# Dealing tokens to partitions in turns of five and four, and moving the left-out-token tables to the last expert

## The chip, the cores and the metric

The kernel runs on one core of a Trainium2 chip. The metric is the device time of one execution in microseconds (us). Before the change three runs gave 597.97 us at the median, between 597.38 and 598.83. A core has a matmul engine (TensorE, PE in the profile, with its weight loads as PEld), a vector engine (DVE), a scalar engine (ACT), GpSimd (POOL) and a sync engine (SP, here used to issue DMA), and 16 DMA engines that all queues share. A difference of about 0.2%, some 1.2 us, is the least that a measurement of this kernel can tell from no change.

## What is computed

A linear attention without softmax, then a top-1 mixture of experts over its output (shapes: 8 batches, 8 heads, 576 tokens a batch, 64 columns a head; 8 experts, 512 to 1,024 and back; a capacity of 1,152 tokens an expert):

```
kv = einsum('bhsd,bhse->bhde', k, v)
out = einsum('bhsd,bhde->bhse', q, kv)
x = out / sqrt(mean(out*out, -1) + 1e-6) * g_norm        # one row of 512 for each of 4,608 tokens
e = argmax(x @ w_gate);  g = softmax(x @ w_gate)[e]      # one expert and one gate for a token
pos = how many earlier tokens chose the same expert       # kept while pos < capacity
y[token] = g * (relu(x @ w1[e]) @ w2[e])                  # 0 for a token that is not kept
```

The position counts tokens in the order of their index, so whatever place a token has in the chip's memory, its index must be known there.

## The kernel before

**Attention.** One batch has 576 = 128 x 4.5 tokens. The kernel gives a batch C = 5 columns on 128 partitions. Column 0 holds tokens 0 to 63 on partitions 0 to 63 (the other half of the column is zero, written once by a memset), columns 1 to 4 hold tokens 64 to 575, four in a row on each of the 128 partitions. k, v and q of half the heads (four of eight) are one load, six loads a batch and 48 in all. `load` issues each as two DMAs on SP's queue:

```
nc.sync.dma_start(h.t[:, :, 1:C], src[b, hs, HP:S].rearrange("h (p c) d -> p h c d", c=C - 1))
nc.sync.dma_start(h.t[0:HP, :, 0], src[b, hs, 0:HP].rearrange("h p d -> p h d"))
```

The first moves 512 pieces of 1,024 bytes, the second 256 pieces of 256 bytes; the pieces are the packets of the profile. Nine buffers (three each for k, v, q) are reused in turn, and every DMA also waits for the one eight before it on its queue. `kv_products` (L700) makes k'v of a batch, `unit` turns q (L764) and multiplies it with kv (L782), `squares` and `route` norm the rows, choose experts and count positions; `place` (L931) counts with ten small matmuls against a triangle `tri16`, `upto16` or `ones16`. `write` (L999, L1001) sends the rows with their logits to `x_dram` from POOL's queue, in two DMAs of 64 and 128 partitions. From batch 3 on the weights of one early expert are loaded and split into a high and a low fp16 part, and the first 384 of its tokens are computed, beside the attention.

**Experts.** For each expert r, `weights` loads w1 and w2 into `raw1` and `raw2`, takes their largest element (DVE `am` L330, `a` L338; a transpose on PE, `across`, L343; DVE `bm` L347; a broadcast on PE, `back`, L350; DVE `bmax` to `sg`), and splits them with that scale (ACT `w1h`, `w2h` L364; DVE `w1l`, `w2l` L370). `rows_beside` gathers the token rows of the next expert (POOL `xg` L426, `xm` L434, ACT `pair` L458, POOL `pair` L462, a DMA transpose from SP), and DVE copies their gates (`gt` L439, which waits for the gather). `products` runs the first GEMM in eight blocks (PE `hp` L515, ACT `hh` L520, DVE `hl` L523), `second` the second one (PE `yp` L561 and L570, ACT `ysb` L586, POOL `out_dram` L591).

**What sets the order.** `Plan` is a small list scheduler in the kernel file: every step has a planned duration, its engines, its dependencies and a key; steps are placed on engines by earliest start and then by key, and the instructions are written in that order. On the chip each engine runs its own list strictly in order. So a step that is placed early on DVE stands ahead of everything placed later, whether or not someone waits for it.

**Left-out tokens.** A fixed budget of rows is computed for each expert. `plan_rest` (L1301 to L1419) makes tables of what a budget or the capacity leaves out, in some 55 small DVE steps; `rest` reads one number from them at the very end and, if it is above zero, runs extra tiles. The steps form one chain on DVE with no dependency ahead of the first, at the key of the last expert:

```
steps, o = plan_rest(), None
for _ in range(60):
    o = op(("V", 0.2), lambda e: next(steps, None), [o], key + 1)
```

Of the kernel before, what the change touches and what calls it, by code (L numbers as in the profile page):

```python
# [11 lines left out]
F32 = mybir.dt.float32  # L12
I32 = mybir.dt.int32
AF = mybir.ActivationFunctionType
ALU = mybir.AluOpType
# [13 lines left out]
NIO = 3  # L29
# [128 lines left out]
def attention_moe_kernel(  # L158
# [12 lines left out]
    nc = tc.nc  # L171
    NB, H, S, D = q.shape
# [3 lines left out]
    P = 128  # L176
    C = 5
    HP = P // 2
    HH = H // 2
    KD = DM // P  # L180
    KF = F // P
    XW = D + E
# [4 lines left out]
    cst = ctx.enter_context(tc.tile_pool(name="cst", bufs=1))  # L187
# [5 lines left out]
    x_dram = dram.tile([N, XR], F32, name="x_dram")  # L193


# [7 lines left out]
    tok_i = cst.tile([P, 2, NT], I32, name="tok_i")  # L203
    by_col = lambda i: tok_i[:, i].rearrange("p (b c) -> p b c", c=C)
    nc.gpsimd.iota(by_col(0), [[S, NB], [1, C]], base=HP, channel_multiplier=C - 1)
    nc.gpsimd.iota(by_col(0)[:, :, 0:1], [[S, NB], [0, 1]], base=1, channel_multiplier=1)
    tok1 = cst.tile([P, NT], F32, name="tok1")
    nc.vector.tensor_copy(tok1, tok_i[:, 0])
# [28 lines left out]
    nc.vector.memset(desc[HP:P, 0], 0.0)  # L237
# [15 lines left out]

    wgs = cst.tile([P, 2, 2, 2, E], F32, name="wgs")
# [5 lines left out]


    kv_bds = []
    for i in range(2):
        t = cst.tile([P, H, 2, XW], F32, name=f"kv_bd{i}")
        nc.gpsimd.memset(t, 0.0)
        kv_bds.append(t)
# [365 lines left out]
    actx = ExitStack()  # L632
    io = actx.enter_context(tc.tile_pool(name="io", bufs=1))
# [6 lines left out]

    ios = {}
    for i in range(NIO):
        for nm, eng in (("k", nc.gpsimd), ("v", nc.vector), ("q", nc.gpsimd)):
            flat = io.tile([P, HH * C * D + D], F32, name=f"{nm}_sb{i}")
            t = flat[:, 0:HH * C * D].rearrange("p (h c d) -> p h c d", h=HH, c=C)
            eng.memset(t[HP:P, :, 0], 0.0)
            if nm == "q":
                eng.memset(flat[:, HH * C * D:], 0.0)
            ios[nm, i] = t, flat
# [21 lines left out]
    def load(b):  # L671
        ts = {}
        for j, (nm, half) in enumerate(ORDER):
            h = new(nm)
            h.t, h.flat = ios[nm, (len(rings[nm].holds) - 1) % NIO]

            def go(e, h=h, src={"k": k, "v": v, "q": q}[nm], hs=slice(half * HH, (half + 1) * HH)):
                nc.sync.dma_start(h.t[:, :, 1:C], src[b, hs, HP:S].rearrange("h (p c) d -> p h c d", c=C - 1))
                nc.sync.dma_start(h.t[0:HP, :, 0], src[b, hs, 0:HP].rearrange("h p d -> p h d"))

            o = op(("S", ISSUE), go, [], (b - 2) * C + j * 0.8, takes=(h,))
            ts[nm, half] = h, op(("D", LOAD), None, [o], takes=(), uses=(h,))
            issued.append(o)
        return ts
# [136 lines left out]
    def route(b, oh, ssh, outs, sums):  # L821
# [26 lines left out]
        o = V(0.1, guess, [o])  # L848
# [74 lines left out]
        def place(e):  # L923
# [4 lines left out]
            terms += [(tri16, rep(ohe[:, c], max(c, 1)), min(c, 1), c + 1) for c in range(C)]  # L928
            terms += [(upto16 if c else ones16, rep(ohe[:, c], C - 1 - c), c + 1, C) for c in range(C - 1)]
# [66 lines left out]
        def write(first):  # L996
            def go(e):
                if first:
# [615 lines left out]
    for r in range(E):  # L1614
# [48 lines left out]
```

## Time and profile before

| | us |
|---|---|
| median of three runs | 597.97 |
| the profiled execution, own time | 593.89 |
| its span, first to last instruction | 592.1 |
| PE busy | 542.7 |
| DVE busy | 384.1 |
| ACT busy | 257.7 |
| POOL busy | 224.0 |

Busy time is the sum over the instructions of an engine. Times of day in the text count from the span's start. The profiled execution is 4.08 us shorter than the median of the runs; a sum made in its rows is taken over to the median as a difference. In the views of the trace, "idle before <- X" is how long an engine stood before an instruction and what ended that, the chain of waits is the work that ended last followed back from the end, and DMA share is the busy time of the 16 DMA engines over the stretch (it can be above 1, since packets overlap).

### The profile page before, as it was taken

To read this page: it belongs to the slowest core of one execution; us is meant where nothing else is said; L and a number is where in the kernel's file an instruction comes from. 1 tells how busy PE (TensorE), PEld (TensorE's weight loads), DVE (VectorE), ACT (ScalarE), POOL (GpSimd) and SP (SyncE) were. 2 spreads that over 40 slices of the span, in tenths; PEclk is the share of its full clock that TensorE was granted. 3 is DMA by queue.
4 is the path that set the end of the run, shared out by engine and by line. 5 is a ranking of instruction groups with operands and counts; after the bars stand their busy time and mean duration, and the time that the engine had idled before them with its cause. 6 is when DMAs were issued, how large, how long until landed. Compare 5 with 4: busy or idle time off the path is not lost.

```text
span 592.1 us, 11996 instructions
## 1 busy us (share of the span) xinstructions
PE 542.7 (92%) x4535; PEld 373.8 (63%) x4535; DVE 384.1 (65%) x1026; ACT 257.7 (44%) x500; POOL 224.0 (38%) x273
## 2 busy tenths in 40 slices
PE   2887999788988979999899999999999999999996
PEld 2787898687534545654575467477558648747843
DVE  2386687999976998899999665648638625201200
ACT  1565676588502652471825252443526435211211
POOL 6002243165334785517522722463274173011011
PEclk9999999988998997999899999999999999999999
DMA  8999999936239669777763752856386143001000
GB/s 225 288 292 329 323 313 356 339 115 232 91 129 346 161 135 244 184 234 228 188 245 103 192 164 90 217 108 216 101 176 206 50 105 73 1 37 38 1 37 29
DMA packets 94654, 102.71 MB, mean 173 GB/s; under 512 B 51650, under 2 KB 76226, under 8 KB 93568
## 3 DMA queue, kind: packets, MB, share of 16 engines
q1 hardware_dynamic: 86528, 70.50, 44.3%
q0 software_dynamic: 8064, 31.40, 15.4%
q8 instruction: 37, 0.61, 0.4%
q14 instruction: 25, 0.20, 0.1%
HBM read 73.20 MB, written 20.68 MB: 159 GB/s over the span
## 4 chain that ended last, share of the span: by engine, by line
PE 41%; DVE 19%; DMA 15%; issue 14%; POOL 4%; ACT 3%; SPq 2%; POOLq 0%; DVEq 0%; ACTq 0%
PE hp L515 17%; PE yp L561 12%; DMA out_dram<-ysb,si 5%; PE op L782 3%; DVE w1l L370 3%; DMA q_sb<-in_q_dram 3%; DVE am L330 3%; DMA v_sb<-in_v_dram 3%; DMA xs<-pair 2%; DMA xg<-x_dram,gi 2%; DVE w2l L370 2%; PE qp L764 2%; PE yp L570 2%; DVE hl L523 2%; PE a L700 2%
## 5 line engine op out<-in xcount | busy, mean ns | idle before, releaser
L515 PE MATMUL hp<-xs,w1h 128*128 128x320 f16 (+6 forms) x960 | 137.1, 296 | 1.6 <-DVE hl L523 0.7
L515 PEld LDWEIGHTS <-w1h 128*128 128x128 f16 x1024 | 100.5, 99 | 38.9 <-issue 4.2
L561 PEld LDWEIGHTS <-hh 128*128 128x128 f16 x560 | 54.2, 98 | 63.7 <-issue 1.9
L591 POOL DMA_INDIRECT out_dram<-ysb,si x42 | 44.7, 1064 | 130.8 <-ACT ysb L586 94.1
L520 ACT ACTIVATE hh<-hp 128x320 f16<-128x320 f32 (+7 forms) x64 | 40.9, 640 | 110.7 <-PE hp L515 108.9
L426 POOL DMA_INDIRECT xg<-x_dram,gi x42 | 43.7, 1040 | 92.5 <-DVE w1l L370 58.2
L330 DVE TENSOR_REDUCE am<-raw 128x1 f32<-128x512 f32 x120 | 75.4, 673 | 0.0
L523 DVE SCALAR_TENSOR_TENSOR hl<-hp,hh 128x320 f16<-128x320 f32 (+7 forms) x64 | 47.4, 741 | 41.0 <-ACT hh L520 40.9
L515 PE MATMUL hp<-xs,w1l 128*128 128x320 f16 (+6 forms) x480 | 72.1, 292 | 0.0
L561 PE MATMUL yp<-w2h,hl 128*128 128x512 f16 x272 | 65.9, 385 | 0.0
L561 PE MATMUL yp<-w2h,hh 128*128 128x512 f16 x272 | 64.9, 379 | 0.8 <-ACT ysb L586 0.8
L782 PE MATMUL op<-kv_bd,qt 128*128 128x144 f32 (+1 forms) x384 | 60.2, 301 | 5.8 <-ACT o_sb L665 2.1
L561 PE MATMUL yp<-w2l,hh 128*128 128x512 f16 x272 | 64.7, 379 | 0.0
L515 PEld LDWEIGHTS <-w1l 128*128 128x128 f16 x512 | 49.9, 98 | 16.6
L782 PEld LDWEIGHTS op<-kv_bd,qt 128*128 128x128 f32 x384 | 52.3, 202 | 9.1 <-ACT o_sb L665 3.3
L458 ACT CAST pair<-xm 128x512 f16<-128x512 f32 (+5 forms) x36 | 22.1, 614 | 81.0 <-POOL xm L434 73.9
L370 DVE SCALAR_TENSOR_TENSOR w2l<-raw,sw,w2h 128x512 f16<-128x512 f32 x64 | 47.6, 793 | 7.7 <-ACT w2h L364 7.7
L462 POOL TENSOR_TENSOR pair<-xm,pair 128x512 f16<-128x512 f32 (+5 forms) x36 | 43.4, 1207 | 23.1 <-ACT pair L458 22.7
L370 DVE SCALAR_TENSOR_TENSOR w1l<-raw,sg,w1h 128x512 f16<-128x512 f32 x64 | 52.0, 853 | 0.0
L586 ACT ACTIVATE ysb<-yp,ysc 128x512 f32<-128x512 f32 (+5 forms) x41 | 27.9, 681 | 51.5 <-PE yp L561 36.7
L561 PEld LDWEIGHTS <-hl 128*128 128x128 f16 x280 | 27.7, 99 | 34.2 <-issue 2.6
L434 POOL TENSOR_TENSOR xm<-xg 128x512 f32<-128x512 f32 (+5 forms) x39 | 43.4, 1114 | 9.6 <-DMA xg<-x_dram,gi 6.1
(242 smaller groups left out, 690.9 us busy)
## 6 DMA issues: line engine op xcount, KB each, us to landing
raw<-in_moe_w_dram SPq DMA_DIRECT2D x64, 512.0 KB
x_dram<-o_sb POOLq DMA_DIRECT2D x8, 1152.0 KB
k_sb<-in_k_dram SPq DMA_DIRECT2D x16, 512.0 KB
v_sb<-in_v_dram SPq DMA_DIRECT2D x16, 512.0 KB
q_sb<-in_q_dram SPq DMA_DIRECT2D x16, 512.0 KB
x_dram<-o_sb POOLq DMA_DIRECT2D x8, 144.0 KB
k_sb<-in_k_dram SPq DMA_DIRECT2D x16, 64.0 KB
v_sb<-in_v_dram SPq DMA_DIRECT2D x16, 64.0 KB
```

Of the source, the lines that this page charges most:

```text
L330: nc.vector.tensor_reduce(out=am()[:, p:p + 1], in_=raw[:, sl(p)], axis=AX.X, op=ALU.max, apply_absolute_value=True)
L370: nc.vector.scalar_tensor_tensor(out=wl[:, sl(p)], in0=raw[:, sl(p)], scalar=z["s"], in1=wh[:, sl(p)], op0=ALU.mult, op1=ALU.subtract)
L426: nc.gpsimd.indirect_dma_start(out=self.xg[i][0:n], out_offset=None, in_=x_dram[0:self.rows, :], in_offset=bass.IndirectOffsetOnAxis(ap=se ...
L434: eng.tensor_tensor(out=self.xm[i][0:n].rearrange("p (h d) -> p h d", h=H), in0=xg[:, :, 0:D], in1=xg[:, :, D:D + 1].broadcast_to([n, H, D ...
L462: nc.gpsimd.tensor_tensor(out=pair[0:n, 1], in0=self.xm[i][0:n], in1=pair[0:n, 0], op=ALU.subtract)
L515: nc.tensor.matmul(self.view(hp)[:, u], lhsT=w[:, c, j * P:(j + 1) * P], rhs=x[:, c, u * hw:(u + 1) * hw], start=(t == 0 and c == 0), stop ...
L520: nc.scalar.activation(self.out(self.hh, j), self.view(hp), AF.Relu)
L523: nc.vector.scalar_tensor_tensor(out=self.out(self.hl, j), in0=self.view(hp), scalar=0.0, in1=self.out(self.hh, j), op0=ALU.max, op1=ALU.s ...
L561: nc.tensor.matmul(yp[0:n, 0:DM], lhsT=h[:, j, o:o + n], rhs=w[:, j, :], start=(m == 0), stop=(m == len(self.terms) - 1))
L586: nc.scalar.activation(self.ysb[0:n], yp[0:n, 0:DM], AF.Copy, scale=self.ysc[0:n, i:i + 1])
L591: nc.gpsimd.indirect_dma_start(out=out[:, :], out_offset=bass.IndirectOffsetOnAxis(ap=self.sidx[0:n, col:col + 1], axis=0), in_=ysb[0:n], ...
L782: nc.tensor.matmul(ph.t[:, j * m:(j + 1) * m], lhsT=qt.t[:, i * P:(i + 1) * P], rhs=x, start=True, stop=True)
```

## The change

**Tokens.** Each pair of partitions now takes nine tokens in a row: the even partition five, the odd one four, in columns 1 to 4, with its column 0 zero. A load is again two DMAs on SP, over the 64 odd partitions (256 pieces of 1,024 bytes) and the 64 even ones (256 pieces of 1,280 bytes); the rows go to `x_dram` in the same two groups. Token numbers, the mask `desc` and the triangle matmuls follow the new order. The zeros of column 0 are now written over all 128 partitions, in front of the first load, which has to wait for them; the buffers' memsets are therefore moved to the head of the program.

**Tables.** The chain of `plan_rest` now depends on `hh[0]`, the first hidden block of the last expert.

```diff
-            eng.memset(t[HP:P, :, 0], 0.0)                       # behind the set-up
+            eng.memset(t[:, :, 0], 0.0)                          # ahead of it
...
-                nc.sync.dma_start(h.t[:, :, 1:C], src[b, hs, HP:S].rearrange("h (p c) d -> p h c d", c=C - 1))
-                nc.sync.dma_start(h.t[0:HP, :, 0], src[b, hs, 0:HP].rearrange("h p d -> p h d"))
+                rows = src[b, hs].rearrange("h (p n) d -> p h n d", n=2 * C - 1)
+                nc.sync.dma_start(h.t[1:P:2, :, 1:C], rows[:, :, C:])
+                nc.sync.dma_start(h.t[0:P:2], rows[:, :, 0:C])
...
-            terms += [(tri16, rep(ohe[:, c], max(c, 1)), min(c, 1), c + 1) for c in range(C)]
-            terms += [(upto16 if c else ones16, rep(ohe[:, c], C - 1 - c), c + 1, C) for c in range(C - 1)]
+            terms += [(tri16, rep(ohe[:, c], c + 1), 0, c + 1) for c in range(C)]
+            terms += [(upto16, rep(ohe[:, c], C - 1 - c), c + 1, C) for c in range(C - 1)]
...
-                    nc.gpsimd.dma_start(x_dram[b * S:b * S + HP], o_sb[0:HP, 0].rearrange("p h x -> p (h x)"))
+                    nc.gpsimd.dma_start(rows[:, C:], o_sb[1:P:2, 1:C].rearrange("p c h x -> p c (h x)"))
...
-                    nc.gpsimd.dma_start(x_dram[b * S + HP:(b + 1) * S].rearrange("(p c) d -> p c d", c=C - 1),
-                                        o_sb[:, 1:C].rearrange("p c h x -> p c (h x)"))
+                    nc.gpsimd.dma_start(rows[:, 0:C], o_sb[0:P:2].rearrange("p c h x -> p c (h x)"))
...
-            steps, o = plan_rest(), None
+            steps, o = plan_rest(), hh[0]
```

Three places in the instruction order carry the prediction. The first is SP's queue at the start of the program: the loads of the first k and v halves, with what each waits for (49 is the end of a semaphore's name; the number behind k_sb is the buffer's). Before:

```order
L678 DMA k_sb_180<-in_k_dram 128x4x256
L679 DMA k_sb_180<-in_k_dram 64x4x64
L678 DMA v_sb_182<-in_v_dram 128x4x256
L679 DMA v_sb_182<-in_v_dram 64x4x64
L678 DMA k_sb_187<-in_k_dram 128x4x256
```

Now:

```order
L684 DMA k_sb_73<-in_k_dram 64x4x256
L685 DMA k_sb_73<-in_k_dram 64x4x320 [waits Pool_49]
L684 DMA v_sb_75<-in_v_dram 64x4x256
L685 DMA v_sb_75<-in_v_dram 64x4x320 [waits DVE_49]
L684 DMA k_sb_80<-in_k_dram 64x4x256
```

The number and order of the DMAs is the same; the second of a load waits for a memset on POOL or DVE.

The second is DVE where it takes the maxima of the fourth expert's weights (the second and third experts are under way): `am`, `a`, `bm` and `sg` are steps of that maximum, `gt` waits for a gather, and `sel`, `big`, `off` and `t_tab` belong to the tables. Before:

```order
L439 COPY gt<-xg 128x1
L330 TENSOR_REDUCE am_3816<-raw_2643 128x1
L1354 TENSOR_TENSOR sel<-iota_77,upto 128x396
L347 TENSOR_REDUCE bm<-pt_max 1x1
...
L1372 SCALAR_TENSOR_TENSOR t_tab<-iota_77,t_tab 128x44
L370 SCALAR_TENSOR_TENSOR w1l_2645<-raw_149,sg,w1h_2644 128x512
L347 TENSOR_REDUCE bm<-pt_max 1x1
L370 SCALAR_TENSOR_TENSOR w1l_2645<-raw_149,sg,w1h_2644 128x512 x4
```

Now:

```order
L456 COPY gt<-xg 128x1
L364 TENSOR_REDUCE bm<-pt_max 1x1
L347 TENSOR_REDUCE am_3792<-raw_2651 128x1
L456 COPY gt<-xg 112x1
...
L355 TENSOR_REDUCE a_1_3872<-am_3792 128x1
L387 SCALAR_TENSOR_TENSOR w1l_2653<-raw_181,sg,w1h_2652 128x512 x3
L364 TENSOR_REDUCE bm<-pt_max 1x1
L387 SCALAR_TENSOR_TENSOR w1l_2653<-raw_181,sg,w1h_2652 128x512 x3
```

The table steps are gone from here; the first `bm` stands right behind the `gt` that waits for the gather, the second `bm` behind three `w1l` instead of one. On POOL, two output writes change places with an `xm` each there; on PE, the broadcast that needs the first `bm` stands eight matmuls earlier.

The third is DVE in the last expert, between the blocks of its first GEMM (`hl`). Before:

```order
L552 TENSOR_SCALAR ysc<-gt,ys 128x4
L552 TENSOR_SCALAR ysc<-gt,ys 32x1
L523 SCALAR_TENSOR_TENSOR hl<-hp,hh 128x544 x7
L576 COPY yt<-yp 128x128
L1422 TENSOR_LOAD n_i
```

Now:

```order
L1360 TENSOR_TENSOR sel<-iota_101,upto 128x396
L540 SCALAR_TENSOR_TENSOR hl<-hp,hh 128x544
L1362 TENSOR_TENSOR big<-iota_101,upto 128x396
L1364 TENSOR_TENSOR sel<-sel,big 128x396
L1370 SCALAR_TENSOR_TENSOR off<-upto,start 128x9
L1372 SCALAR_TENSOR_TENSOR off<-ent,off 128x9
L1374 TENSOR_TENSOR big<-sel,off 128x396
L1376 TENSOR_REDUCE t_tab<-big 128x44
L1378 SCALAR_TENSOR_TENSOR t_tab<-iota_101,t_tab 128x44
L540 SCALAR_TENSOR_TENSOR hl<-hp,hh 128x544
```

The chain of table steps now stands among these seven blocks, five to nine steps in a gap; the last two steps stand behind them. The gap that holds the most work is the one with the seven steps from `big` to `t_tab`.

## Rows read from the trace of the kernel before

**Rows 1.** The page, its head and busy times.

```profile
span 592.1 us, 11996 instructions
PE 542.7 (92%) x4535; PEld 373.8 (63%) x4535; DVE 384.1 (65%) x1026; ACT 257.7 (44%) x500; POOL 224.0 (38%) x273
```

**Rows 2.** Busy time by stretch (columns PE, PEld, DVE, ACT, POOL, clock, DMA).

```profile
30.00:40.00 10.00, 9.33 (x131) 8.76 (x131) 8.36 (x25) 6.57 (x16) 0.00 (x0) 0.97 1.14 292
...
290.00:310.00 20.00, 20.00 (x150) 14.45 (x149) 19.70 (x41) 9.57 (x15) 4.91 (x5) 1.00 0.82 253
```

**Rows 3.** The chain of waits, first 75 us (start, us, what).

```profile
18.40 7.66 DMA v_sb<-in_v_dram
26.20 1.71 PE a L700 x40
...
49.46 7.74 DMA q_sb<-in_q_dram
...
59.98 10.19 DMA q_sb<-in_q_dram
70.30 0.63 PE qp L764 x4
```

**Rows 4.** DMA queue from 20.5 to 21 us (packets, MB, share).

```profile
DMA packets 152, 0.15 MB, mean 309 GB/s; under 512 B 1, under 2 KB 152, under 8 KB 152
q1 hardware_dynamic: 152, 0.15, 108.9%
```

**Rows 5.** The same from 21.4 to 21.9 us.

```profile
DMA packets 250, 0.15 MB, mean 301 GB/s; under 512 B 152, under 2 KB 249, under 8 KB 249
q1 hardware_dynamic: 249, 0.13, 112.0%
```

**Rows 6.** The same from 103.5 to 106 us, weight loads.

```profile
DMA packets 370, 1.03 MB, mean 410 GB/s; under 512 B 32, under 2 KB 149, under 8 KB 370
q1 hardware_dynamic: 370, 1.03, 102.3%
```

**Rows 7.** The first instructions, timeline (start, us, engine, line, what).

```profile
1.23 0.74 SPq L679 DMA_DIRECT2D k_sb<-in_k_dram  x1
...
6.27 0.31 POOL L646 MEMSET k_sb<- 64x256 f32 x1
```

**Rows 8.** Who PE waited for, 185 to 592 us (us, times, longest).

```profile
PE yp L581 <- DVE t_e L1315: 4.7, 1, 4.7
PE pt_max L350 <- DVE bm L347: 3.0, 2, 2.7
PE hp L515 <- DVE hl L523: 0.7, 1, 0.7
```

**Rows 9.** DVE's timeline, 275 to 285 us.

```profile
275.35 0.15 DVE L439 COPY gt<-xg 128x1 f32<-128x1 f32 x1 [1.17 <-DMA xg<-x_dram,gi]
...
276.02 0.56 DVE L1354 TENSOR_TENSOR sel<-iota,upto 128x396 f32<-128x396 f32 x1
276.50 0.27 DVE L347 TENSOR_REDUCE bm<-pt_max 1x1 f32<-1x128 f32 x1
...
283.63 0.73 DVE L1372 SCALAR_TENSOR_TENSOR t_tab<-iota,t_tab 128x44 f32<-128x44 f32 x1
```

**Rows 10.** PE's timeline in the same place.

```profile
276.82 0.38 PE L350 MATMUL pt_max<-bm,ones 1*128 1x1 f32 x2 [0.30 <-DVE bm L347]
...
285.27 0.38 PE L350 MATMUL pt_max<-bm,ones 1*128 1x1 f32 x2 [2.68 <-DVE bm L347]
```

**Rows 11.** POOL's timeline in the same place.

```profile
276.62 1.01 POOL L591 DMA_INDIRECT out_dram<-ysb,si  x1 [2.39 <-DMA out_dram<-ysb,si]
277.65 1.08 POOL L434 TENSOR_TENSOR xm<-xg 128x512 f32<-128x512 f32 x1
```

**Rows 12.** ACT's timeline in the same place.

```profile
282.48 3.17 ACT L364 ACTIVATE w1h<-raw,sg 128x512 f16<-128x512 f32 x5
```

**Rows 13.** DVE's timeline in the last expert.

```profile
555.03 0.72 DVE L523 SCALAR_TENSOR_TENSOR hl<-hp,hh 128x544 f16<-128x544 f32 x1 [2.06 <-ACT hh L520]
```

More of the change, by code (lines that the diff above doesn't have):

```diff
@@ L193, in attention_moe_kernel @@
     x_dram = dram.tile([N, XR], F32, name="x_dram")
+    actx = ExitStack()
+    io = actx.enter_context(tc.tile_pool(name="io", bufs=1))
+    ios = {}
+    for i in range(NIO):
+        for nm, eng in (("k", nc.gpsimd), ("v", nc.vector), ("q", nc.gpsimd)):
+            flat = io.tile([P, HH * C * D + D], F32, name=f"{nm}_sb{i}")
+            t = flat[:, 0:HH * C * D].rearrange("p (h c d) -> p h c d", h=HH, c=C)
+            eng.memset(t[:, :, 0], 0.0)
+            if nm == "q":
+                eng.memset(flat[:, HH * C * D:], 0.0)
+            ios[nm, i] = t, flat
     ident = cst.tile([P, P], F32, name="ident")
@@ L236, in attention_moe_kernel @@
     nc.vector.tensor_copy(desc, desc8.rearrange("p (o e) -> p o e", o=1).broadcast_to([P, C, E]))
-    nc.vector.memset(desc[HP:P, 0], 0.0)
+    even = cst.tile([P, 1], F32, name="even")
+    nc.vector.tensor_scalar(out=even, in0=pair[:, 0:1], scalar1=-1.0, scalar2=1.0, op0=ALU.mult, op1=ALU.add)
+    nc.vector.tensor_scalar(out=desc[:, 0], in0=desc8, scalar1=even, scalar2=None, op0=ALU.mult)
     rbud = cst.tile([P, E], F32, name="rbud")
@@ L252, in attention_moe_kernel @@
         nc.gpsimd.dma_start(gcol[h2 * D:(h2 + 1) * D], g_norm.rearrange("(d o) -> d o", o=1))
+    kv_bds = []
+    for i in range(2):
+        kv_bds.append(cst.tile([P, H, 2, XW], F32, name=f"kv_bd{i}"))
+    for t in kv_bds:
+        nc.gpsimd.memset(t, 0.0)
     wgs = cst.tile([P, 2, 2, 2, E], F32, name="wgs")
@@ L259, in attention_moe_kernel @@
     nc.vector.tensor_scalar(out=wgs, in0=wgs, scalar1=gcol, scalar2=None, op0=ALU.mult)
[L262 to L266, printed above, removed]
     mv_all = cst.tile([P, NT], F32, name="mv_all")
@@ L629, in slots @@
         return both
-    actx = ExitStack()
-    io = actx.enter_context(tc.tile_pool(name="io", bufs=1))
     at = actx.enter_context(tc.tile_pool(name="at", bufs=2))
@@ L639, in attention_moe_kernel @@
     tab, misc = bank("tab"), bank("misc")
[L641 to L645, printed above, removed]
-            eng.memset(t[HP:P, :, 0], 0.0)
-            if nm == "q":
-                eng.memset(flat[:, HH * C * D:], 0.0)
-            ios[nm, i] = t, flat
     o_sbs, sss = [], []
@@ L997, in go @@
             def go(e):
+                rows = x_dram[b * S:(b + 1) * S].rearrange("(p n) d -> p n d", n=2 * C - 1)
                 if first:
-                    nc.gpsimd.dma_start(x_dram[b * S:b * S + HP], o_sb[0:HP, 0].rearrange("p h x -> p (h x)"))
+                    nc.gpsimd.dma_start(rows[:, C:], o_sb[1:P:2, 1:C].rearrange("p c h x -> p c (h x)"))
                 else:
-                    nc.gpsimd.dma_start(x_dram[b * S + HP:(b + 1) * S].rearrange("(p c) d -> p c d", c=C - 1),
-                                        o_sb[:, 1:C].rearrange("p c h x -> p c (h x)"))
+                    nc.gpsimd.dma_start(rows[:, 0:C], o_sb[0:P:2].rearrange("p c h x -> p c (h x)"))
             return go
```

13 lines of the change are left out of this document (9 added, 4 removed).

## Prediction

> **What bounds the kernel now.** I read the busy times first: PE works 542.7 of 592.1 us [rows 1], so apart from PE's own work only some 50 us can be won, and the question is where they lie. Busy time by stretch answers that for both ends. In 30 to 40 us the DMA engines are full (share 1.14 at 292 GB/s) and PE still has gaps, while from 290 us on PE is busy for all of its time [rows 2]: what this change removes there is worth nothing, and what it adds costs only if PE is made to wait. The chain of waits then says which loads count. Up to the `v` half whose DMA is issued at 18.40 and done 7.66 us later, at 26.06, the loads set the pace; its end is what PE's next products start from [rows 3]. From there to 49.46 the chain runs over PE and DVE, then it enters two more `q` loads (7.74 and 10.19 us from issue to landing), and from 70.30 on no load stands in it [rows 3]. The list of those for whom PE waits after 185 us holds one large item, 4.7 us for a step `t_e` of the tables, and 3.0 us in two pieces for `bm` [rows 8].
>
> **Loads: what one costs.** A load is 589,824 bytes (128 x 4 x 1,024 + 64 x 4 x 256); at 292 GB/s that is 2.02 us, and 10 loads have landed by 26.06. The change keeps the bytes and turns 512 packets of 1,024 and 256 of 256 bytes into 256 of 1,024 and 256 of 1,280. So I need a price for each size. A stretch with 152 packets of 1,024 bytes has a share of 108.9% of 16 engines over 0.5 us, 8.71 us of engine time, or 57.3 ns a packet [rows 4]. The next has 97 of these and 152 small ones in 112.0%, 8.96 us; less 97 x 57.3 it leaves 3.40 us, 22.4 ns a small one [rows 5]. Weight loads have 221 of 4,096 bytes, 117 taken at 57.3 and 32 at 22.4 in 102.3% of 2.5 us, 40.92 us: 152 ns for 4,096 bytes [rows 6]. The price of another byte is therefore 0.045 ns between 256 and 1,024 bytes and 0.031 above it. A packet of 1,280 bytes, which this trace does not have, comes to 65 to 69 ns. Before, a load holds each engine for (512 x 57.3 + 256 x 22.4) / 16 = 2.19 us, after it for (256 x 57.3 + 256 x 65 to 69) / 16 = 1.96 to 2.02: 0.17 to 0.23 us less, and over a share of 1.12 to 1.14 (packets overlap) 0.15 to 0.21 us of time. I take 0.15, the price nearest to the 1,024-byte row. The ends: nothing, if the bytes and not the packets set the 2.02 us; 256 x 22.4 / 16 / 1.12 = 0.32, if the small packets go and 256 further bytes on a packet are free. That 4,096-byte packets move 410 GB/s [rows 6] speaks against the lower end.
>
> The row of small packets says that one takes 0.39 of the time of a 1,024-byte packet for a quarter of its bytes [rows 5]. [...]
>
> **Loads: how many count.** Ten up to 26.06, then those that land in the two stretches of the chain. 7.74 us are 3.8 loads of 2.02; the second stretch holds 2.45 us more, in which `x_dram` rows of the first batch share the queue, and otherwise as many. The first load of each has been running for a part of its time when the chain enters, so I count 3.5 for each, 7 for both. That is 17 x 0.15 = **2.6 us** (ends 0 and 5.4). Loads between 28 and 47 us land while PE and DVE set the pace, so they are costed at nothing.
>
> **The start.** The first `k` half no longer needs zeros behind it but ahead of it: its second DMA waits for a memset, a wait that holds SP's queue and with it all later loads. The memsets, which now begin only at 6.27 on POOL (0.31 us each) [rows 7], stand at the head of the program; the first is done about when the second DMA of the load was issued, 1.23 [rows 7]. I cost it at 0, with 0.3 us (one memset) to either side. What they push back on POOL, the identity and the gate weights, is wanted only after 15 us. The `x_dram` writes keep their bytes in packets that are all above 9,000 bytes, and the wider triangle matmuls are a few columns: both 0.
>
> **Tables: what they held up.** The steps moved stand on DVE between 184 and 333 us. At the fourth expert's maxima eight of them, from `sel` (0.56) at 276.02 to `t_tab` (0.73) at 283.63, sum to 5.9 us [rows 9]; behind the last stands the `bm` for which PE waits 2.68 us [rows 10]. A sum that stopped here would book 2.68. But what is late next? In the new order the second `bm` stands behind three `w1l`, which need `w1h`; ACT begins these at 282.48, five in 3.17 us [rows 12], so the third ends at 284.4 and its `w1l` near 285: no gain at all as the times stand. `w1h` waits for a cast behind POOL's output write, which stood 2.39 us for the write before it, with `xm` behind [rows 11]. The new order puts an `xm` ahead of that write, which frees the casts by about 1.6 us (1.01 of the write and part of its wait). So the second `bm` wins about **1.5 us**.
>
> The first `bm` stands right behind `gt`, which waited 1.17 us for its gather and ran at 275.35 [rows 9]. PE's broadcast, which came to it at 276.52 and waited 0.30 [rows 10], stands eight matmuls earlier, and PE will be there some 1.7 us sooner. The gather does not move with it. Small savings before this place (`hl` 0.7 and the first `bm` 0.30 [rows 8, 10], and some 0.4 of `yp`'s 4.7, the table step that the list names last; the rest of the 4.7 is `w2l` on DVE, which stays) are 1.4 us, and a new wait of about 1.8 us here eats them. I book the two at 0 together. The ends for the tables: 2.68 + 1.4, about 4 us won, if gather and casts come with PE; 0.7 us lost, if the new wait stands whole against half of the small savings and the second `bm` wins nothing.
>
> **Tables: where they go.** In the last expert `hl` runs every 2.78 us for 0.72 us, and DVE is idle 2.06 us between [rows 13]. The gap from `big` to `t_tab` has seven steps, 3.1 us if `big`, `off` and `t_tab` run like their neighbours of the same shape, 5.3 us as they ran beside POOL (POOL has nothing but seven issues there). So `hl` can come 1.1 us late, but it is read only by the second GEMM and by the buffer of a block two further on, which leaves about 1.4 us: 0, with 1.8 us at the worst price. The last two steps are behind the last `hl`, with PE's second GEMM still to run.
>
> **Sum.** 2.6 + 1.5 = 4.1 us less: 593.89 becomes 589.8 in the profiled execution, and, as a difference, 597.97 becomes **593.9**.
>
> **The rivals.**
> *(A) The loads do not get shorter*, because bytes set their pace, or because the hardware cuts 1,280 bytes into 1,024 and 256, in which case the packets are those of before and the change does not do what it says. For it: the share is above 1 all through [rows 2], so a packet's time is partly queueing. Against it: the rows of larger packets. It gives 597.97 - 1.5 = 596.5. [...]
> *(B) The tables' gain is lost whole:* the broadcast waits for the gather, the second `bm` for three `w1l`, as long as before. For it: the rows of `gt` and `w1h` [rows 9, 12]. Against it: POOL's new order. 597.97 - 2.6 = 595.4.
> *(C) Slower: packets that begin at multiples of 256 bytes cost more.* The pieces now start every 2,304 bytes, no longer every 1,024. If each costs what a large and a small one cost together, 79.7 ns, a load holds an engine 2 x 256 x 79.7 / 16 = 2.55 us in place of 2.19, 0.32 us more over the share: 17 x 0.32 = 5.4 us lost, less 1.5: 601.9. It decides once a packet of 1,280 and one of 1,024 bytes take over 137 ns together (2 x 57.3 + 22.4); in the sum they take 122 to 126. Against it: before, the 256-byte packets and large ones side by side show no such price [rows 5].
> *(D) Both gains in full:* 5.4 + 4, 588.6.
>
> **How the numbers follow.** The forecast has 0.45, A 0.17, B 0.18, C 0.10, D 0.10. A difference of 0.2%, 1.2 us, is about what a measurement of this kernel can tell. The forecast gives 0.40 faster, 0.04 the same, 0.01 slower; A, 1.5 us under the old median, is split 0.08, 0.07 and 0.02; B 0.12, 0.06 and 0 (the start and the last expert can cost it its margin); C all slower; D all faster: 0.70, 0.17 and 0.13. The range leaves out C and the edge of D and takes in A with 1.8 us of the last expert and the start's 0.3 on top: 588.5 to 599.5.
>
> **What would show it.** Up to 26 us: the last of ten loads done near 24.6, and engine time of a load near 2.0 us; 26.1 says A, over 28 says C. No table step on DVE before 540 us; the second `bm`'s broadcast with a wait near 1 us and the first with one near 1.8. In the last expert `hl` late by up to a microsecond, and no wait of PE. PE busy without a gap from 290 on. It would be wrong if SP stood waiting for a memset, if casts still held the second `bm`, or if the new order put some wait elsewhere among the second to fourth experts, where DVE's, POOL's and PE's lists are dealt anew.

## The result

The changed kernel takes 591.36 us at the median of nine runs (589.6 to 594.63), the kernel before 597.97 in nine runs beside it (596.29 to 599.99). The ratio is 0.9894 with a 95% interval of 0.9872 to 0.9915, 5.1 to 7.7 us less. The forecast was 593.9 with a range of 588.5 to 599.5, and faster with a chance of 0.70. The direction and the range held and the gain was 6.6 us where 4.1 were forecast, but three of the steps that led to it were wrong, and that the sum came this near is in part luck. The rest of the text is about these. Ratios leave out executions more than 1.5% above the fastest of their kernel; medians leave out none.

The head of the page of after (first line the span, then busy time of each engine), which answers to [rows 1]:

```profile
span 588.8 us, 12003 instructions
PE 540.6 (92%) x4535; PEld 373.1 (63%) x4535; DVE 382.6 (65%) x1031; ACT 258.0 (44%) x500; POOL 221.5 (38%) x273
```

All busy times are as before to within 2.5 us. Of the 3.3 us by which the span is shorter, 2.1 are PE's own busy time, although it runs the same 4,535 matmuls; the rest is waiting that went. Over whole executions the clock that was granted to TensorE is the same (as a share of the full clock, a median of 0.978 in 63 executions of the kernel before over all series, 0.976 in 15 of the changed one), so it does not carry the gain; between two single traces it can, as a place below shows. This execution took 590.7 us, 0.7 under its median; that of before lay 4.1 under its own. Two traces set side by side therefore show only 3.2 us, and small differences are read below from several of each kind.

Busy time by stretch (PE, PEld, DVE, ACT, POOL, clock, DMA share, GB/s), the same two stretches as [rows 2]:

```profile
30.00:40.00 10.00, 8.09 (x130) 7.33 (x129) 8.97 (x35) 5.92 (x16) 0.00 (x0) 1.00 1.00 324
290.00:310.00 20.00, 20.00 (x148) 14.34 (x147) 17.85 (x38) 4.32 (x7) 4.12 (x5) 1.00 0.41 139
```

The DMA engines move 324 GB/s where they moved 292, with a lower share; the late stretch is full of PE as it was. For whom PE waits on loads up to 185 us (us in all, times, longest), in before:

```profile
PE a L700 <- DMA v_sb<-in_v_dram: 4.0, 2, 2.0
PE qp L764 <- DMA q_sb<-in_q_dram: 3.9, 3, 2.3
```

and in after:

```profile
PE misc L937 <- DVE ohe L913: 3.8, 4, 1.9
PE a L706 <- DMA v_sb<-in_v_dram: 1.8, 1, 1.8
```

7.9 us of waiting for loads became 1.8; the `q` loads are no longer waited for at all, and what took their place in part is `ohe`, a step of the routing on DVE (1.9 us before). From 185 us on PE's waits of after are these (line numbers are 17 higher than before's here):

```profile
PE yp L598 <- DVE gt L456: 5.8, 1, 5.8
PE pt_max L367 <- DVE bm L364: 2.5, 2, 2.1
PE hp L532 <- DVE p2t L312: 1.3, 2, 0.9
```

Against [rows 8], the 4.7 us before `yp` are now 5.8, and the two waits for `bm` are 2.5 in place of 3.0. The place on which the prediction booked 1.5 us, the second `bm`, gave 0.5 (2.68 became 2.14).

### The profile page after: what moved, and what is told of

Same layout as the page of the kernel before. It is cut to its first block, busy times and chain, and to the rows that moved or that the text cites. A ratio compares the mean times of both kernels' runs of the same rounds, so it can differ in the third digit from the quotient of the medians.

```text
span 588.8 us, 12003 instructions
## 1 busy us (share of the span) xinstructions
PE 540.6 (92%) x4535; PEld 373.1 (63%) x4535; DVE 382.6 (65%) x1031; ACT 258.0 (44%) x500; POOL 221.5 (38%) x273
## 4 chain that ended last, share of the span: by engine, by line
PE 38%; issue 17%; DVE 16%; DMA 10%; POOL 5%; ACT 4%; POOLq 0%; SPq 0%; DVEq 0%; ACTq 0%
PE hp L532 19%; PE yp L578 8%; DMA out_dram<-ysb,si 8%; PE op L788 4%; DVE w1l L387 3%; DVE w2l L387 3%; DVE am L347 2%; PE qp L770 2%; POOL pair L479 2%; DVE hl L540 1%; DMA xg<-x_dram,gi 1%; PE a L706 1%; PE yp L587 1%; POOL xm L451 1%; DMA raw<-in_moe_w_dram 1%
## 5 line engine op out<-in xcount | busy, mean ns | idle before, releaser
L532 PE MATMUL hp<-xs,w1l 128*128 128x320 f16 (+6 forms) x480 | 72.1, 292 | 0.0
L578 PE MATMUL yp<-w2h,hl 128*128 128x512 f16 x272 | 64.3, 379 | 0.0
```

Of the source, the lines that this page charges most:

```text
L532: nc.tensor.matmul(self.view(hp)[:, u], lhsT=w[:, c, j * P:(j + 1) * P], rhs=x[:, c, u * hw:(u + 1) * hw], start=(t == 0 and c == 0), stop ...
L578: nc.tensor.matmul(yp[0:n, 0:DM], lhsT=h[:, j, o:o + n], rhs=w[:, j, :], start=(m == 0), stop=(m == len(self.terms) - 1))
```

## Where the time went, over several traces

PE runs the same 4,535 matmuls in all these kernels, in nearly the same order, so the start of the n-th matmul is a clock that can be compared. Taken from the traces, the time from the span's start to matmul 720 (k, v and q of the first batches), from there to 1,560 (end of the attention), to 2,640 (the first experts), to 4,080 and to the last, in us:

```
                              to 720   to 1560   to 2640   to 4080   to the last
before                         76.07    103.79    171.11    186.88     48.36
before, second trace           77.65    104.09    172.54    188.21     47.59
before + tables moved          77.18    104.14    168.82    189.37     47.59
after, tables not moved        75.56    103.54    174.45    190.73     47.59
after                          71.75    105.32    168.40    189.05     48.29
after, second trace            72.39    104.52    169.76    190.07     47.59
```

The old loads (three rows) need 77.0 us on average to matmul 720, the new ones 73.2 (72.1 without the row of the layout alone, which was 2.0 to 2.6 us behind the other two at matmul 120). Three traces of experiments below agree: 76.82 with the old loads, 71.94 with the new ones, and 71.98 with small pieces on the even partitions. From there to 1,560 the new loads give back 0.5 us (104.5 against 104.0). Tables in their old place need 172.7 from 1,560 to 2,640, moved ones 169.0. From 2,640 to 4,080 the moved ones lose 0.9 us (189.5 against 188.6, and of the latter one row is 190.7). That makes 3.8 - 0.5 + 3.7 - 0.9 = 6.1 us, near the 6.6 measured; each term stands on three traces a side that differ among themselves by 1 to 4 us.

The 3.7 us of the tables can be split by place. By the same count of matmuls, from 1,560 on, in us; the last row is the experiment with a third `pair` buffer, further down:

```
                          to 1,860   to 1,980   to 2,280   to 2,640
before                       49.97      18.05      44.53      58.56
before, second trace         50.16      18.16      45.44      58.79
after, tables not moved      47.95      23.62      44.31      58.57
before + tables moved        48.71      17.20      44.35      58.57
after                        48.18      17.20      44.46      58.57
after, second trace          48.58      17.20      43.78      60.21
before + third buffer        49.27      17.19      41.55      58.79
```

The second column is where PE waits for `hl` in the second expert. Moved tables need 17.20 there in every trace, 0.9 us less than before, and 6.4 less than the layout alone. The first column looks like a gain of 1.3 to 2.0 us over before, but it is the clock: the kernel with the layout alone has its tables in the old place and is as fast there as the rest. Busy time from 180 to 190 us (the column behind the five engines is the clock) in before, its second trace, the layout alone and after:

```profile
180.00:190.00 10.00, 7.17 (x33) 3.46 (x31) 6.74 (x18) 2.12 (x4) 3.90 (x5) 0.83 1.01 358
```

```profile
180.00:190.00 10.00, 7.79 (x33) 3.35 (x31) 6.61 (x21) 1.86 (x4) 3.90 (x4) 0.83 0.96 336
```

```profile
180.00:190.00 10.00, 7.25 (x46) 4.21 (x44) 8.39 (x21) 1.98 (x4) 4.64 (x5) 1.00 0.99 370
```

```profile
180.00:190.00 10.00, 7.85 (x52) 5.09 (x53) 9.76 (x27) 2.92 (x6) 3.98 (x4) 1.00 1.02 402
```

In both traces of before, 3.4 of these 10 us run at the lower of the two clock levels (0.50 of the full clock in place of 1.00), right behind a wait of 2.2 us for `xm`; eight `yp` matmuls take 3.32 us there and 1.89 elsewhere. The other five rows have nearly the same wait (1.9 to 2.5 us) and no such fall. Why only these two have it is not shown, so this part is not to be credited to the tables. What the traces show of the tables' gain is thus 0.9 us against before, at `hl`, some tenths at the second `bm`, and 6.4 at `hl` against the one trace that has the shorter loads without them.

## The experiments

**One part of the change alone.** Theory L was that the loads carry the gain, rival T that the tables do.

```diff
-            steps, o = plan_rest(), hh[0]
+            steps, o = plan_rest(), None
```

> The changed kernel with the chain of table steps without a dependency, as before; the new token layout and loads stay. Theory L (the loads carry the gain): the 4.3 us that PE is ahead at 70 us in the trace of the changed kernel stay, so 4 to 5.5 us under the kernel before (592.5 to 594), and the 2.7 us wait of the second maximum's broadcast is still there near 281 us. Rival T (the tables carry most of the 6.6 us): under 3 us gained, 595 or more.

Measured: 595.78 us, ratio 0.9975 (0.9941 to 1.001).

```diff
-            steps, o = plan_rest(), None
+            steps, o = plan_rest(), hh[0]
```

> The kernel before with the table steps behind the last expert's first hidden block and nothing else changed. Theory L: 1 to 2 us gained (596 to 597), PE level with the kernel before up to 185 us and ahead from about 215 us, by up to 1.5 us. Rival T: 3 us or more gained (595 or less). Rival B of the prediction (the tables give nothing): within 0.7 us of the kernel before.

Measured: 594.58 us, ratio 0.9943 (0.9899 to 0.9987). Both medians came out on rival T's side of its bounds, though 594.58 only just. By the ratios the layout alone is worth 1.5 us (a loss of 0.6 to a gain of 3.5) and the tables alone 3.4 (0.8 to 6.0), so the tables carry at least as much as the loads; the loads' part by itself can't be told from nothing by this measurement. Beside these, in the same series, the changed kernel has 590.23 us and all executions of the kernel before 598.3: by these medians the loads are worth 2.5 us without the tables and 4.4 with them, the tables 3.7 without the loads and 5.6 with them. Together they would give more than the two alone, though 590.23 rests on six executions. The trace of the layout alone suggests why; its execution took 599.7 us, 3.9 above its median, so its waits are on the long side. PE reaches matmul 720 ahead of before (75.56 us), and then, in the second expert, stands 4.79 us for a block. PE and ACT there, timeline of this kernel (start, us, engine, line, operation, and in brackets the idle time and what ended it):

```profile
242.12 3.92 PE L532 MATMUL hp<-xs,w1h 128*128 128x336 f16 x16 [4.79 <-DVE hl L540]
```

```profile
230.53 0.73 ACT L537 ACTIVATE hh<-hp 128x672 f16<-128x672 f32 x1 [2.18 <-PE hp L532]
239.93 0.62 ACT L475 CAST pair<-xm 128x512 f16<-128x512 f32 x1 [8.67 <-DMA xs<-pair]
240.46 1.34 ACT L537 ACTIVATE hh<-hp 128x672 f16<-128x672 f32 x2
```

ACT's list has a `pair` cast ahead of two `hh`. The cast needs one of two `pair` buffers, and these come free when a DMA transpose has read them, here after 8.67 us of waiting. The `hh` behind it had its products long before (PE had ended those of the first by 234 us); `hl` waits for `hh`, and PE for `hl`. The kernel before has the same row with a shorter wait (line 17 lower):

```profile
238.62 0.62 ACT L458 CAST pair<-xm 128x512 f16<-128x512 f32 x1 [4.58 <-DMA xs<-pair]
239.14 0.72 ACT L520 ACTIVATE hh<-hp 128x672 f16<-128x672 f32 x1
```

In after the planner, with the tables out of DVE's way, has put the third `hh` ahead of the cast:

```profile
232.15 0.73 ACT L537 ACTIVATE hh<-hp 128x672 f16<-128x672 f32 x1 [2.69 <-PE hp L532]
234.40 0.62 ACT L475 CAST pair<-xm 128x512 f16<-128x512 f32 x1 [1.51 <-DMA xs<-pair]
```

**The same two kernels again.** 

> The kernel before, unchanged, for a second trace of it. The profiled execution of before was 4.1 us under its median and that of the changed kernel only 0.7 under its own, so the two traces differ by 3.2 us where the medians differ by 6.6. If the first trace was a lucky one, this one comes out at 596 to 599 us and shows stretches at the lower clock, or a scatter to the output, that took longer than in the first. If it again comes out near 594, the profiler itself shortens the kernel before, and the traces, not the medians, would have to be explained.

Measured: 598.5 us at the median, ratio 1.0032 (0.9996 to 1.0068), this profiled execution 597.84. The first trace was a lucky one, as the first branch of the expectation has it.

> The changed kernel, unchanged, beside the others on the same chip: 5.0 to 7.7 us under the kernel before, as measured. In the first trace it lost 1.5 us to the kernel before between 111 and 138 us (PE at the lower clock) and 2.3 us between 440 and 455 us (behind a scatter to the output of 8.8 us). If these are accidents of one execution they are absent or elsewhere in this trace; if the change brings them, both are here again.

Measured: 590.23 us, ratio 0.9883 (0.9827 to 0.9938). The loss between 111 and 138 us is all but absent (0.2 us). That between 440 and 455 us is here again, and 1.5 us of it also in the second trace of before, in that with the tables alone and in that with the layout alone. So the change does not bring that part; the first trace of before lacks it. In the second trace of before, POOL and then PE:

```profile
440.77 1.02 POOL L591 DMA_INDIRECT out_dram<-ysb,si  x1 [4.34 <-DMA xs<-pair]
```

```profile
455.41 2.12 PE L515 MATMUL hp<-xs,w1h 128*128 128x288 f16 x16 [0.88 <-DVE p2t L295]
```

and in after:

```profile
432.82 1.01 POOL L608 DMA_INDIRECT out_dram<-ysb,si  x1 [5.11 <-DMA xs<-pair]
```

```profile
447.46 2.12 PE L532 MATMUL hp<-xs,w1h 128*128 128x288 f16 x16 [0.91 <-DVE p2t L312]
```

An output write stands on POOL for 4.3 to 5.1 us, the `xm` behind it comes late, the casts and `w2h` on ACT behind that, and `w2l` on DVE holds `hl`. This is where the moved tables lose the 0.9 us between matmul 2,640 and 4,080; that it is due to PE being earlier is not shown, since the loss does not follow PE's lead from trace to trace.

**What holds a load.** The first four kernels here are for the loads alone: what they leave out or misplace changes the routing and so all that follows, and their whole times say nothing. A load is done when the last of its DMA completions is in the trace.

The kernel before without the 256-byte pieces (tokens 0 to 63 of each batch are left out):

```diff
-                nc.sync.dma_start(h.t[0:HP, :, 0], src[b, hs, 0:HP].rearrange("h p d -> p h d"))
```

> The kernel before without the second DMA of each load: tokens 0 to 63 of each batch are left out, column 0 stays zero, 512 packets of 1,024 bytes are left. Read as the time between loads done, with four in flight: 2.07 us before, 1.64 after the change. Theory P (a packet has a price of its own, and the small ones cost more than I took, 0.46 us a load by the times at which the DMAs are done): 1.6 us a load. By the prices of the prediction (0.32 us for the small ones): 1.75. Rival Y (bytes alone set the pace): 2.07 x 524,288 / 589,824 = 1.84.

The changed kernel with the halves of the partitions in place of odd and even ones (rows land on other partitions):

```diff
-                nc.sync.dma_start(h.t[1:P:2, :, 1:C], rows[:, :, C:])
-                nc.sync.dma_start(h.t[0:P:2], rows[:, :, 0:C])
+                nc.sync.dma_start(h.t[HP:P, :, 1:C], rows[:, :, C:])
+                nc.sync.dma_start(h.t[0:HP], rows[:, :, 0:C])
```

> The changed kernel with its two DMAs a load on partitions 64 to 127 and 0 to 63 in place of the odd and the even ones; packets, bytes and queue are the same, the rows land on other partitions, so the routing that follows is another one and only the loads are compared. Theory P: the time between loads done stays at 1.64 us. Rival S (the gain comes from spreading each DMA over all partitions by turns): 1.9 us or more.

The changed kernel with one DMA a load, in 1,152-byte and in 2,304-byte packets (in both, tokens land cut up and the output is another):

```diff
+                nc.sync.dma_start(h.t.rearrange("p h c d -> p h (c d)")[:, :, D // 2:],
+                                  src[b, hs].rearrange("h s d -> h (s d)").rearrange("h (p x) -> p h x", p=P))
```

> The changed kernel with one DMA a load over all 128 partitions, 512 packets of 1,152 bytes, the same bytes; tokens land cut up, so only the loads are compared. Theory P: as many packets and bytes as in the changed kernel, 1.6 to 1.7 us a load. Rival S, turned round (two DMAs over half the partitions each are dearer than one): 1.55 or less. Rival Y: 1.64 as well.

```diff
+                nc.sync.dma_start(h.flat[:, 0:HH * C * D].rearrange("p (g x) -> p g x", g=2)[:, :, D:],
+                                  src[b, hs].rearrange("(g i) s d -> g (i s d)", g=2).rearrange("g (p x) -> p g x", p=P))
```

> The changed kernel with one DMA a load, 256 packets of 2,304 bytes, the same bytes; tokens land cut up, so only the loads are compared. Theory P: half the packets again; from the 0.165 us that 256 packets take longer for 256 more bytes each (0.91 against 0.75 us), a packet of 2,304 bytes is 0.75 + 5 x 0.165 = 1.57 us for 256, so 1.5 to 1.57 a load. Rival Y: 1.64 as now.

And last, the whole computation again: the changed kernel with the packets of before, but with tokens 0 to 63 on the even partitions in place of partitions 0 to 63.

```diff
-                nc.sync.dma_start(h.t[1:P:2, :, 1:C], rows[:, :, C:])
-                nc.sync.dma_start(h.t[0:P:2], rows[:, :, 0:C])
+                nc.sync.dma_start(h.t[:, :, 1:C], src[b, hs, HP:S].rearrange("h (p c) d -> p h c d", c=C - 1))
+                nc.sync.dma_start(h.t[0:P:2, :, 0], src[b, hs, 0:HP].rearrange("h p d -> p h d"))
```

> The changed kernel, tables and memsets included, with the packets of before: 512 of 1,024 bytes over 128 partitions and 256 of 256 bytes for tokens 0 to 63, but these on the even partitions in place of partitions 0 to 63 (token numbers, mask, triangle and writes follow). The run with the lower and the upper half of the partitions took 2.74 us a load where the odd and even ones take 1.66, so the partitions of a DMA matter. Rival S (what made the loads of before slow is that the small DMA reaches partitions 0 to 63 only): 1.6 to 1.7 us between loads done, and the changed kernel's time, 590 to 592. Theory P (the 256-byte packets themselves): 2.0 to 2.05 us, and 2 to 4 us over the changed kernel, 593 to 595. In between, both have a share.

Measured, the median time between two loads done, from the fifth to the seventeenth load:

```
                                                us    packets of a load (bytes), partitions
before                                         2.06   512 (1,024) all; 256 (256) 0 to 63
before without the small ones                  1.50   512 (1,024) all
after                                          1.66   256 (1,024) odd; 256 (1,280) even
after, by halves                               2.74   256 (1,024) 64 to 127; 256 (1,280) 0 to 63
after, small ones on the even partitions       1.80   512 (1,024) all; 256 (256) even
one DMA, 1,152 bytes                           1.50   512 (1,152) all
one DMA, 2,304 bytes                           1.51   256 (2,304) all
```

Rival S is right about the halves: the same packets, bytes and queue take 1.08 us more when each DMA reaches only 64 neighbouring partitions, where theory P expected no change. Without the small DMA a load takes 1.50 us, less than any of the three expected values, so in before the small pieces cost 0.56 us a load (0.49 by the fastest of the other traces); as one DMA it takes 1.50 too, as the rival turned round has it. With one DMA a load, up to eight loads in place of four can be in the queue at once; the DMA engines are full either way (shares of 1.00 to 1.14 from 16 to 34 us), and this was not separated. The stretch from 28 to 34 us of each (columns as above) shows the DMA engines as busy and moving less; after, by halves, and small ones on even partitions, in this order:

```profile
28.00:34.00 6.00, 5.33 (x60) 4.94 (x58) 5.35 (x14) 4.31 (x12) 0.00 (x0) 1.00 1.08 356
```

```profile
28.00:34.00 6.00, 4.17 (x92) 3.72 (x90) 1.97 (x3) 2.67 (x6) 0.00 (x0) 1.00 1.13 216
```

```profile
28.00:34.00 6.00, 5.33 (x56) 4.97 (x56) 5.19 (x14) 4.49 (x12) 0.00 (x0) 1.00 1.12 328
```

So a packet has no price of its own: at a share of 1.13 over 2.74 us, 512 packets hold 16 engines for 97 ns each by halves, and at 1.08 over 1.66 us for 56 ns spread. The packet records of the traces (16 to 34 us) say it directly. A packet of 1,024 bytes takes 62 ns on average in before, 51 without the small DMA, 53 with the small pieces on the even partitions, 50 in after and 86 by halves; one of 1,280 bytes takes 61 in after, one of 256 bytes 19.5 in before and 18.1 on the even partitions. So the small pieces on partitions 0 to 63 make the large ones beside them longer by 9 to 12 ns each, and the small DMA of before is slow for both reasons. Spread over the even partitions, the same 256-byte packets bring a load from 2.06 to 1.80 us; taken together with the 1,024-byte ones into fewer packets, to 1.66. Of the 0.40 us that a load became shorter, 0.26 is the partitions and 0.14 the packets. Three more traces with the loads of before give 1.99 to 2.04 us and three more with the changed ones 1.65 to 1.66, so the partitions' part can be as little as 0.19. The packets' part rests on two kernels and on a difference of 0.14 which stands in at least ten of the twelve intervals of each (1.59 to 1.68 us against 1.74 to 1.82).

Why it matters which partitions a DMA reaches is not shown by these runs. They show that it does: from 28 to 34 us 216 GB/s were moved by halves, 356 with the odd and the even partitions, and 328 with the small pieces on the even ones.

In all, the kernel with the small ones on the even partitions takes 589.72 us (ratio 0.9858, 0.9829 to 0.9887), level with the changed kernel's 0.9883 to 0.9894, although its loads are 0.14 us slower each. PE reaches matmul 720 at 71.98. Turns of five and four are therefore not needed for the time: dealing the first 64 tokens to every other partition does as much.

**The cast in front of the block.** If ACT's order is what the tables win in the second expert, a third `pair` buffer should win it too, in the kernel before:

```diff
-            self.pair[i] = self.pool.tile([P, 2, DM], F16, name="pair", bufs=2)
+            self.pair[i] = self.pool.tile([P, 2, DM], F16, name="pair", bufs=3)
...
-("xm", 1), ("pair", 2),
+("xm", 1), ("pair", 3),
```

> The kernel before with three buffers in place of two for the row pairs in the expert stage (the ring and the tile); on ACT this moves one pair cast of the second expert's rows behind the hidden block that stood behind it, the same place where moving the tables did it. Theory O (what the tables win beyond DVE's own time is this order: ACT's cast waits for a transpose with a hidden block behind it): the wait of ACT near 240 us no longer stands before a hidden block, PE 0.9 us sooner between 230 and 245 us and more where the transpose is slow, in all 1 to 2 us under the kernel before. Rival D (the tables win by DVE's time alone): PE level with the kernel before there, within 0.5 us in all.

Measured: 592.87 us at the median of its six runs, 5.7 under the 598.54 beside it. The ratio, 0.983 (0.976 to 0.99), rests on three of the six and makes the gain look larger. ACT's list changes at that place alone, those of the other engines not at all, and it reads

```profile
237.22 0.73 ACT L520 ACTIVATE hh<-hp 128x672 f16<-128x672 f32 x1 [2.18 <-PE hp L515]
238.72 0.62 ACT L458 CAST pair<-xm 128x512 f16<-128x512 f32 x1 [0.76 <-DMA xs<-pair]
240.64 0.73 ACT L520 ACTIVATE hh<-hp 128x672 f16<-128x672 f32 x1 [1.31 <-PE hp L515]
```

No `hh` waits behind a cast there any more, and PE needs 17.19 us from matmul 1,860 to 1,980, the same as with the tables moved: on what ACT's order is worth at that place, 0.9 us, theory O holds, and rival D is out. But the kernel gains more than the 1 to 2 us expected: from matmul 1,560 to 2,640 this trace needs 166.80 us, 4.3 and 5.7 less than the two of before. Some 0.7 to 0.9 us of the rest is the fall of the clock near 186 us, which this trace does not have. The larger part lies at the second `bm` of the fourth expert's maxima,

```profile
282.98 0.38 PE L350 MATMUL pt_max<-bm,ones 1*128 1x1 f32 x2 [1.11 <-DVE bm L347]
```

for which PE waits 1.11 us in place of 2.68 [rows 10]. Near it both traces of before have another 3.4 us at the lower clock (the clock from 268 to 296 us is 0.94 in both), this one has none (1.00). That one buffer does this with the tables still in DVE's way shows that these were not all that held it; which earlier transpose or write set it free, and whether the clock follows from the shorter wait, was not followed up.

> The changed kernel with three buffers for the row pairs. Theory O: the cast stands behind the hidden block already, so at most 0.5 us more from later casts that wait for transposes, and the dealing of ACT's list is another one: within 1.5 us of the changed kernel. If casts elsewhere still hold PE, 2 us or more under it.

Measured, with the same two lines in the changed kernel: 589.85 us, ratio 0.9888 (0.9837 to 0.994), level with the changed kernel, as the first branch says. None of these versions beats it by more than can be measured here.

## The prediction, step by step

**What bounds the kernel** held: the gain lies ahead of 290 us, and from there PE gives back little but at the place near 447 us.

**The price of a load** was mis-sized: 0.15 us less a load was taken, 0.40 measured, above even the upper end of 0.32. The step that failed is the working from packet prices. I priced a 256-byte packet at 22.4 ns from its share of the engines [rows 5] and a 1,280-byte one from the 1,024-byte row [rows 4], as if size alone set a price. A small packet on partitions 0 to 63 stretched the large ones beside it, so that part of its cost stood in the price of the large ones, which the sum left unchanged: they fell from 62 to 50 ns. (The trace's records also show that the packets under 512 bytes were not all of 256: 16 of the 152 in [rows 5] and the 32 of [rows 6] have 4 bytes.) With the records' own averages a load holds each engine for 2.30 us in before and 1.77 in after, and over shares of 1.13 and 1.08 that is 2.04 and 1.64 us, close to the measured 2.06 and 1.66. In after 200 packets of a stretch, all but 11 of them of 1,024 or 1,280 bytes, have

```profile
DMA packets 200, 0.22 MB, mean 359 GB/s; under 512 B 11, under 2 KB 200, under 8 KB 200
q1 hardware_dynamic: 200, 0.22, 110.0%
```

110.0% of 16 engines over 0.6 us: 10.56 us, or 55 ns each for 1,139 bytes on average, less than I took for 1,024 bytes alone. The rows shown of before could not separate size from place, since there every small packet went to partitions 0 to 63.

**How many loads count** was too many: 17 x 0.40 would be 6.8 us, and PE is ahead by 3.8 to 4.9. Up to 26 us it went as forecast (the tenth load done at 24.27 against 24.6 forecast and 26.06 before), but after that PE and DVE are late next: the waits for `q` were gone before the shorter loads had given all they could. The two errors cancel in part, 2.6 us forecast and 3.8 measured at matmul 720; that these two are near each other is luck.

**The start** held: the first matmul starts at 9.22 and 8.59 us in the two traces of after, 8.65 and 11.12 in those of before. SP stood for a memset by no more than the 0.3 us that were allowed (the second DMA starts at 1.53 us in place of 1.23 [rows 7], the eighth at 5.47 in place of 5.25):

```profile
0.72 0.75 SPq L684 DMA_DIRECT2D k_sb<-in_k_dram  x1
1.53 0.61 SPq L685 DMA_DIRECT2D k_sb<-in_k_dram  x1
2.19 0.61 SPq L684 DMA_DIRECT2D v_sb<-in_v_dram  x1
```

**The tables' gain** was put at the wrong place. By the whole times it is 3.4 us (0.8 to 6.0), not 1.5, and only 0.5 of it is seen at the second `bm`. There rival B's mechanism is what happened, nearly whole. PE and DVE of after:

```profile
269.77 0.38 PE L367 MATMUL pt_max<-bm,ones 1*128 1x1 f32 x2 [0.40 <-DVE bm L364]
...
279.41 0.38 PE L367 MATMUL pt_max<-bm,ones 1*128 1x1 f32 x2 [2.14 <-DVE bm L364]
```

```profile
269.38 0.15 DVE L456 COPY gt<-xg 128x1 f32<-128x1 f32 x1 [2.58 <-DMA xg<-x_dram,gi]
...
275.91 3.25 DVE L387 SCALAR_TENSOR_TENSOR w1l<-raw,sg,w1h 128x512 f16<-128x512 f32 x3 [2.35 <-ACT w1h L381]
279.08 0.27 DVE L364 TENSOR_REDUCE bm<-pt_max 1x1 f32<-1x128 f32 x1
```

The second `bm` waits for three `w1l`, these for `w1h`, and DVE is idle 2.35 us before them. The step that failed is "which frees the casts by about 1.6 us". The write of [rows 11] does stand behind its `xm` now, and no longer waits; but the output write ahead of it, which before waited 0.79 us, stands for longer than the 2.39 us of [rows 11]:

```profile
266.47 1.03 POOL L608 DMA_INDIRECT out_dram<-ysb,si  x1 [4.11 <-DMA out_dram<-ysb,si]
```

POOL waits there for the end of an earlier output write, and with it wait the gather, the `xm` and the casts behind. The new wait for the first `bm`, forecast at about 1.8 us, is 0.40, so the small savings ahead of it were not eaten; but of these the 0.4 at `yp` was wrong, that wait is 1.1 us longer (5.8 against 4.7). What gain the traces show is at a place that the prediction counted as "`hl` 0.7" [rows 8] and did not follow back: this was PE behind `hl`, `hl` behind `hh`, and `hh` behind the cast. For the trace of before 0.7 was about right (0.9 measured). The prediction did not ask what this wait becomes when PE comes there sooner, as shorter loads make it, or a transpose is slow: 4.79 us in the one trace with the layout alone. Where the rest of the 3.4 us lies stays open.

**The last expert** held as worked out. The seven steps of the fullest gap run 3.1 us together, and `hl` comes 1.0 us late (551.67 + 2.78 is 554.45), with no wait of PE behind it; from matmul 4,080 on, moved and unmoved tables take 47.59 us alike in two traces of each:

```profile
551.67 0.72 DVE L540 SCALAR_TENSOR_TENSOR hl<-hp,hh 128x544 f16<-128x544 f32 x1 [0.54 <-ACT hh L537]
552.31 0.56 DVE L1362 TENSOR_TENSOR big<-iota,upto 128x396 f32<-128x396 f32 x1
...
555.32 0.20 DVE L1378 SCALAR_TENSOR_TENSOR t_tab<-iota,t_tab 128x44 f32<-128x44 f32 x1
555.45 0.72 DVE L540 SCALAR_TENSOR_TENSOR hl<-hp,hh 128x544 f16<-128x544 f32 x1
```

**The rivals.** A is out: loads are shorter, and 1,280 bytes are no pair of packets (the records of after have them whole, at 61 ns each). B was right in its mechanism at the second `bm` and wrong in its price, since it left out the gain at `hl`. C is out: nothing became dearer by starting at multiples of 256 bytes; its point of decision, 137 ns for two packets, compares with 111 measured (50 and 61). D, both gains larger, is the nearest of the four in size: 588.6 against 591.36, with other reasons.

## What to carry to other kernels

Ask of a DMA which partitions it reaches before pricing its packets: here a remainder that went to every other partition cost less than one that filled the lower half (1.80 us a load against 2.06), and this could be had without changing the packets. When an instruction list is dealt by a planner, the cost of a waiting instruction is what stands behind it on its engine (in the kernel with the layout alone a cast waited 8.67 us on ACT, two `hh` stood behind it, and PE stood 4.79 us), so a wait of an engine that looks idle (ACT was busy 44% of the span) is to be followed back from the engine that bounds, and asked again for the times that the change brings. Look at the granted clock before you credit a faster stretch to the change: 3.4 us at the lower level cost PE some 1.5 us here. And a single trace can be 4 us to one side of its median: where a step is worth 2 us, several traces of each kernel are needed to place it.

## What the runs showed that was not expected

- The same 512 packets of a load take 1.66 us on odd and even partitions and 2.74 us on the two halves (216 GB/s in place of 356).
- One DMA over all partitions takes 1.50 us for 512 packets of 1,152 bytes and 1.51 for 256 of 2,304, but also 1.50 for 512 of 1,024, which are 11% fewer bytes. Neither bytes nor packets alone set that pace; what does was not settled.
- A DMA transpose of one row tile took 15.97 us in the kernel with the layout alone, where four weight loads were issued from 223 to 241 us; the chain of waits has it in one piece. In the five traces that show it, the two at this place take 6.6 to 16.0 us, and most of the others near it 2 to 5.

```profile
223.86 15.97 DMA xs<-pair
```
